# A linear-attention and gated-unit layer on one core: rewritten engine orders, in which x of tiles 0 and 1 is asked for between the two parts of the value weights

## The chip, the core and the metric

The kernel runs on one core of a Trainium2 chip. Its time is in device microseconds (us). The median of three runs before the change is 283.45 us (283.43 to 284.15). One more execution was profiled; all rows of the profile are of that one.

## The reference

There are 2048 rows of x with 640 columns, all in bf16, and 32 heads of 20.

```python
x = A_x
h = x + A(layernorm(x), A_wqkv, A_w_phi, A_wo)
h2 = h + B(layernorm(h), B_w_gate, B_w_up, B_w_down)

# A: q, k, v = x @ wqkv, by heads
pq = einsum("bhsd,hdf->bhsf", q, w_phi); pk = the same of k
phi_q = concat(softmax(pq), softmax(-pq)); phi_k = the same of pk
kv = einsum("bhsf,bhsd->bhfd", phi_k, v); z = sum of phi_k over s
o = (phi_q @ kv) / (phi_q @ z + 1e-6); result o @ wo

# B: ((x @ w_gate) * (x @ w_up)) @ w_down
```

## The kernel before, in words

The rows are worked in 16 tiles of 128. Because the sum over phi_k needs all rows, the kernel first makes keys and values of all tiles, then the sum, then queries, attention output and the gated unit, in four blocks of four tiles.

The layer norm is folded into the weights. For the keys and the queries the product of wqkv's part with the block-diagonal w_phi (tile `Phi`) is made first, and each row's mean is taken out of the weights. The names that matter here are those of the units in the written orders:

- `in`: the first loads. They are w_phi (`Wrows`), the five blocks of key weights into `Wnat` (called c0 to c4 below; a part of the tile `phiqT`), the value weights into `Wp` in two parts (blocks 0-1 and blocks 2-4), and x of tiles 0 to 3, transposed while it is loaded, into `xT` (x0 to x3 below).
- `wk` and `x0` to `x4`: the key weights. Each block c is summed over its columns for the mean (`means`) and transposed on TensorE (`turn`, line 656); then five rounds multiply it with `Phi` and write `Wp`.
- `wv` and `c0` to `c4` in the DVE order: column sums of the value weights, in the two parts, and the taking out of the mean.
- `s0`, `s2`, `s4`, `s8`, `s12`: mean and square sum of the tiles of x, by two or four tiles. `s2` needs x2 and x3.
- `wm` and `y0` to `y4`: the means of the query weights (`wq_means`, line 721), and five rounds with `Phi` (`wq_round`, line 728). They need `lwq`, the query weights in `Wnat`, and `t0` to `t4`, the same weights transposed by load into `WT`.
- `k`, `v`, `q`: ten matmuls of 320 columns for a tile's keys, values or queries; `K` and `Q` the rest of their softmax, with a large product on POOL each; `A` the sum over phi_k on TensorE.
- `n`, `h`, `f`, `d`, `e`: attention, output product, gated unit, down product.
- `lT4` to `lT15`: transposed loads of x for the other tiles. `lx0` to `lx3`: plain loads of x, four tiles each. `lg`, `lu`, `ld`: the gate, up and down weights, 1.92 MB each. `lwo`: the output weights, 0.8 MB.

What sets the order of the work: `ORDER` (line 58) holds a written list of units for each of the engines PE, DVE, ACT, POOL and SP. An engine issues its operations exactly in that list's order; operations of one unit on one engine are taken in the order in which the program makes them. `Prog.place` (line 200) walks the lists with a model of durations; from the walk come the buffer numbers and the slots of the DMA semaphores. The model's landing time of a load does not change the list. `Prog.finish` adds the waits. Loads go round a ring of eight semaphores (`"w"` for plain loads, `"tr"` for transposing loads), so a load waits for the eighth one before it on its ring. An engine that waits for an operation at the head of its list issues nothing behind it, and that holds for SP's loads too.

SP's list before begins with eleven `in` units (the five key blocks, the two value parts, x0 to x3), then `lT4 lT5 lT7 lT6 lx3 lT8 ...`. Loads issued by SP have line 465 (plain) and line 469 (transposing) in the profile before; matmuls made by the helper `mms` have line 568.

Of the kernel before, what the change touches and what calls it, by code (L numbers as in the profile page):

```python
# [5 lines left out]
FP32 = mybir.dt.float32  # L6
# [5 lines left out]
P = 128  # L12
# [60 lines left out]
    "DVE":  # L73
# [12 lines left out]
    "ACT":  # L86
# [9 lines left out]
    "POOL":  # L96
# [37 lines left out]
class Op:  # L134
    __slots__ = ("eng", "idx", "emit", "deps", "dma", "waits", "vc", "signal", "tick", "sem", "val",
                 "n", "dur", "lat", "bufs", "succ", "start", "end", "open", "bytes", "unit")


class Prog:
# [13 lines left out]
    def op(self, eng, emit, rd=(), wr=(), app=(), dma=None, t=0.2, lat=None, use=(), after=(), size=0.0):  # L153
        o = Op()
        o.eng, o.emit, o.dma = eng, emit, dma
# [44 lines left out]
    def place(self):  # L200
# [20 lines left out]
        while len(order) < len(ops):  # L221
# [29 lines left out]
            if o.dma is not None:  # L251
                land = max(s + 2.3, fabric) + o.bytes
                fabric = land
                o.end = land + o.lat
                flight.setdefault(o.dma[0], []).append(o.end)
            else:
                o.end = s + o.lat
# [119 lines left out]
def _build(ctx, nc, A_x, A_wqkv, A_w_phi, A_wo, B_w_gate, B_w_up, B_w_down, out):  # L377
# [43 lines left out]
    nmean = sb([P, NC], FP32, "nmean")  # L421
    Ssum = sb([P, 2, 2 * H], FP32, "Ssum")
# [9 lines left out]
    nmu, nmuk = [outb[:, k, :].rearrange("p (a n) -> p a n", a=NC) for k in range(2)]  # L432
# [31 lines left out]
    def load(out_, in_, wr, mb, after=(), eng="SP", app=()):  # L464
        return g.op(eng, lambda e: e.dma_start(out_, in_), wr=wr, app=app, after=after, dma=("w", 8), t=0.5, lat=0.4, size=mb / 0.38)  # L465

    def transpose(out_, in_, rd, wr, use=(), t=1.27, size=1.07):

        return g.op("SP", lambda e: e.dma_start_transpose(out_(), in_()), rd=rd, wr=wr, use=use, dma=("tr", 8), t=t, lat=0.5,  # L469
                    size=size)  # L470
# [27 lines left out]
    def load_wnat(w, cs=(0, NC), eng="SP"):  # L498
        c0, c1 = cs
        load(Wnat[:, c0:c1, :], A_wqkv[P * c0:P * c1, D * w:D * (w + 1)].rearrange("(c p) n -> p c n", p=P), R_Wnat[c0:c1],  # L500
             0.16 * (c1 - c0), eng=eng)

    def load_xT(t):
        transpose(lambda: xT[:, t, :, 0:P], lambda: A_x[0, P * t:P * (t + 1), :], [], [R_xT[t]], t=1.27, size=0.8 if t < 2 else 1.4)

    def load_x(b):
        load(x_all[:, 4 * b:4 * b + 4, :], A_x[0, 4 * P * b:4 * P * (b + 1), :].rearrange("(t p) n -> p t n", p=P), [R_x[b]], 0.64)

    def load_wv(c0, c1):
        load(Wp[:, c0:c1, 2 * D:3 * D], A_wqkv[P * c0:P * c1, 2 * D:3 * D].rearrange("(c p) n -> p c n", p=P), R_Wp[2][c0:c1], 0.16 * (c1 - c0))  # L510

    U("in")
    load(Wrows[:, :, :], A_w_phi.rearrange("h d f -> (h d) f").rearrange("(a p) f -> p a f", p=P), [R_Wrows], 0.03, eng="ACT")
    for c in range(NC):
        load_wnat(1, (c, c + 1))
    load_wv(0, 2)
# [587 lines left out]
```

## Time and profile before

| what | us |
|---|---|
| median of three runs | 283.45 |
| the profiled execution | 281.24 |
| its span, first to last instruction | 279.42 |
| TensorE busy | 274.6 |
| TensorE's first long run begins | 13.70 |
| last matmul done | 275.99 |
| DVE / ACT / POOL busy | 165.5 / 133.4 / 106.3 |

The page of the profile gives busy times, the span in 40 slices, the DMA queues, the chain of work that ended last, and the costliest groups. The chain of waits is followed back from the last instruction: at each step to what released it, or to the instruction before it on its engine. SPq is SyncE issuing a DMA. In a line of the list of waits the three numbers are the microseconds in all, how often, and the longest. In a line of the DMA issues the last number is the median time from issue to landing. In a line of the timeline the first two numbers are the start and the length in us.

### The profile page before, as it was taken

Reading aid. Unit: us, or ns where it says so; the run is one execution under the profiler, and the core shown is the slowest. Engines: PE = TensorE matmul, PEld = TensorE weight load, DVE = VectorE, ACT = ScalarE, POOL = GpSimd, SP = SyncE. Lnnn points to the kernel's source line nnn. Section 1 sums busy time; section 2 is a strip of 40 time slices with the busy share of each in tenths; the row PEclk is TensorE's granted clock in tenths of the full one; section 3 lists DMA queues with packets and bytes.
Section 4 is the critical chain, followed back from the end, with each engine's and each line's share of the span. In section 5 each row is a group of like instructions: output and inputs, shape, how many; then the busy total and the mean of one; then the engine's idle time right before and its main releaser. Section 6 shows DMA issues by size and latency. Waiting matters only on the chain.

```text
span 279.4 us, 5540 instructions
## 1 busy us (share of the span) xinstructions
PE 274.6 (98%) x2257; PEld 187.7 (67%) x2257; DVE 165.5 (59%) x313; ACT 133.4 (48%) x227; POOL 106.3 (38%) x156
## 2 busy tenths in 40 slices
PE   8999999999999999999999999999999999999996
PEld 7777778778878888877746655676454444456773
DVE  2999999999899798688528474431141132315011
ACT  2477999998566346363271432401444342410321
POOL 5348899999620322233300680002521034000321
PEclk9999999999999999999999999999999999999999
DMA  7989989404964378946530065561210001000112
GB/s 192 166 170 140 214 125 397 137 2 94 302 78 94 74 180 150 280 99 91 122 73 2 7 136 72 116 98 45 72 49 0 0 0 49 0 0 2 70 48 72
DMA packets 65241, 28.08 MB, mean 100 GB/s; under 512 B 55744, under 2 KB 63936, under 8 KB 65216
## 3 DMA queue, kind: packets, MB, share of 16 engines
q1 hardware_dynamic: 64560, 27.70, 45.8%
q8 instruction: 18, 0.29, 0.5%
q10 hardware_dynamic: 656, 0.03, 0.2%
q14 instruction: 7, 0.06, 0.1%
HBM read 11.82 MB, written 2.62 MB: 52 GB/s over the span
## 4 chain that ended last, share of the span: by engine, by line
PE 94%; SPq 3%; DMA 2%; DVE 1%; issue 0%
PE ps L568 93%; SPq L469 2%; DMA xT<-in_A_x_dram 2%; SPq L465 1%; PE ps L480 0%; DVE outb L1010 0%; DVE KVsb L893 0%; DVE rden L927 0%; DVE KVsb L896 0%
## 5 line engine op out<-in xcount | busy, mean ns | idle before, releaser
L568 PE MATMUL ps<-phik,Wgu 128*128 128x512 bf16 (+1 forms) x600 | 107.6, 336 | 0.0
L568 PEld LDWEIGHTS ps<-phik,Wgu 128*128 128x128 bf16 x600 | 58.2, 98 | 43.6 <-DVE phik L969 1.2
L969 DVE TENSOR_TENSOR phik<-ps,gate 128x512 bf16<-128x512 f32 (+1 forms) x60 | 34.0, 575 | 61.2 <-PE ps L568 60.3
L568 PE MATMUL ps<-Wp,xT 128*128 128x320 bf16 x480 | 68.4, 299 | 0.0
L967 ACT ACTIVATE gate<-ps 128x512 bf16<-128x512 f32 (+1 forms) x60 | 30.1, 512 | 70.4 <-PE ps L568 56.5
L568 PE MATMUL ps<-vaug,phik 128*128 128x320 bf16 (+3 forms) x544 | 60.2, 270 | 0.0
L568 PEld LDWEIGHTS ps<-Wp,xT 128*128 128x128 bf16 x480 | 46.2, 98 | 17.1
L568 PEld LDWEIGHTS ps<-vaug,phik 128*128 128x128 bf16 x544 | 43.4, 97 | 15.9
L985 POOL TENSOR_TENSOR outb<-t,x_all 128x640 bf16<-128x640 f32 x12 | 16.8, 1397 | 88.0 <-ACT t L982 85.7
L827 POOL TENSOR_TENSOR phik<-phik,Rk 128x1280 bf16<-128x1280 bf16 x16 | 37.3, 2357 | 0.7 <-DVE nb L809 0.6
L982 ACT ACTIVATE t<-ps,mh,rs 128x640 f32<-128x640 f32 x12 | 10.6, 882 | 41.4 <-PE ps L568 41.4
L806 DVE TENSOR_REDUCE ps<-ps 128x1 f32<-128x640 f32 x32 | 26.2, 819 | 3.5 <-PE ps L568 3.1
L846 DVE TENSOR_REDUCE Sq<-eq 128x64 f32<-128x1280 bf16 x16 | 23.5, 1474 | 1.6 <-ACT eq L813 1.6
L824 DVE TENSOR_REDUCE Ssum<-phik 128x64 f32<-128x1280 bf16 x16 | 23.4, 1471 | 0.1
L857 POOL TENSOR_TENSOR eq<-eq,rq 128x640 bf16<-128x640 bf16 x16 | 20.3, 1270 | 0.9
L852 POOL TENSOR_TENSOR rq<-Sq,rq 128x32 f32<-128x32 f32 x16 | 4.0, 255 | 39.8 <-DVE rq L851 39.8
L813 ACT ACTIVATE eq<-ps,nb,rs 128x640 bf16<-128x640 f32 x16 | 14.1, 883 | 10.1 <-DVE nb L809 9.3
L813 ACT ACTIVATE phik<-ps,nb,rs 128x640 bf16<-128x640 f32 x16 | 14.0, 884 | 3.1 <-DVE nb L809 3.0
L561 ACT ACTIVATE junk<-x_all 128x640 bf16<-128x640 bf16 x20 | 14.7, 735 | 0.0
L833 ACT ACTIVATE vaug<-ps,rs 128x640 bf16<-128x640 f32 x16 | 12.8, 801 | 3.5 <-PE ps L568 3.5
L813 ACT ACTIVATE eq<-ps,nb,nrs 128x640 bf16<-128x640 f32 x16 | 14.1, 882 | 0.0
L946 DVE SCALAR_TENSOR_TENSOR x_all<-ps,mh,x_all 128x640 bf16<-128x640 f32 x16 | 13.9, 874 | 0.4
(83 smaller groups left out, 226.4 us busy)
## 6 DMA issues: line engine op xcount, KB each, us to landing
x_all<-in_A_x_dram SPq DMA_DIRECT2D x4, 640.0 KB, 9.0
out_dram<-outb SPq DMA_DIRECT2D x15, 160.0 KB, 1.8
Wgu<-in_B_w_up_dram SPq DMA_DIRECT2D x1, 1920.0 KB, 11.3
Wgu<-in_B_w_gate_dram SPq DMA_DIRECT2D x1, 1920.0 KB, 8.2
vaug<-in_B_w_down_dram SPq DMA_DIRECT2D x1, 1920.0 KB, 8.5
phiqT<-in_A_wqkv_dram SPq DMA_DIRECT2D x5, 160.0 KB, 3.8
phiqT<-in_A_wqkv_dram SPq DMA_DIRECT2D x1, 800.0 KB, 6.0
Wo<-in_A_wo_dram SPq DMA_DIRECT2D x1, 800.0 KB, 5.6
```

The source lines that it names most:

```text
L561: g.op("ACT", lambda e: e.activation(out=junk[:, v.i, :], in_=in_, func=func, accum_out=acc), rd=rd, wr=wr, use=[v], t=0.73, lat=0.97)
L568: ins = e.matmul(o_, lhsT=l_, rhs=r_, start=s_, stop=p_, skip_group_check=True)
L806: g.op("DVE", lambda e: e.tensor_reduce(out=mx(), in_=PS[v.i][:, :, 0:HALF], axis=AX.XY, op=ALU.max, apply_absolute_value=True, negate=Tru ...
L813: g.op("ACT", lambda e, s=s, sc=sc: e.activation(out=signed(dst(), s), in_=PS[v.i][:, :, 0:HALF].rearrange("p b (h f) -> p b h f", f=DH), ...
L824: g.op("DVE", lambda e: e.tensor_reduce(out=Ssum[:, vs.i, :], in_=x, axis=AX.X, op=ALU.add), rd=R_phik[t], wr=vs.R, use=[vs], t=1.39, lat=1.5)
L827: g.op("POOL", lambda e: e.tensor_tensor(out=x, in0=x, in1=Rk[:, vr.i, :].unsqueeze(2).to_broadcast([P, 2 * H, DH]), op=ALU.mult), rd=vr.R ...
L846: g.op("DVE", lambda e: e.tensor_reduce(out=Sq[:, vs.i, :], in_=eq[:, b.i, :].rearrange("p (g f) -> p g f", f=DH), axis=AX.X, op=ALU.add), ...
L857: return e.tensor_tensor(out=x, in0=x, in1=rq[:, vr.i, :].unsqueeze(2).to_broadcast([P, H, DH]), op=ALU.mult)
L946: g.op("DVE", lambda e: e.scalar_tensor_tensor(out=xv, in0=PS[v.i][:, :, 0:HALF], scalar=mh[:, t:t + 1], in1=xv, op0=ALU.subtract, op1=ALU ...
L967: g.op("ACT", lambda e: e.activation(out=gate[:, vg.i, 0:P * n], in_=PS[v.i][:, 0, 0:P * n], func=ACT.Copy), rd=[v.R[0]], wr=vg.R, use=[v, ...
L969: g.op("DVE", lambda e: e.tensor_tensor(out=hhT[:, hb, ft, sl], in0=PS[v.i][:, 1, 0:P * n], in1=gate[:, vg.i, 0:P * n], op=ALU.mult), rd=[ ...
L985: g.op("POOL", lambda e: e.tensor_tensor(out=outb[:, vo.i, :], in0=t32[:, v3.i, :], in1=x_all[:, t, :], op=ALU.add), rd=v3.R + [R_h[t]], w ...
```

## The change

1. All five written lists in `ORDER` are new.
2. The first loads are made in another order, and key blocks 2 and 3 go as one load over ACT's queue. In the program x of tiles 0 and 1 now stands between the two parts of the value weights. In SP's new list the eleven `in` units are nine, and they no longer stand together at its head.
3. `load` and `transpose` take a landing time `at`; where it is given, the planner's model uses it as the landing, whenever the load is issued. (`at` stands in the model alone.)
4. `lwq`, `lwo` and the last `lx` are issued by ACT instead of SP.
5. The mean of the query weights: ACT writes five numbers (`nmeanq`) instead of a 640-wide tile, five operations on POOL (`wq0` to `wq4`) add them to the transposed weights, and the rounds `y` on TensorE leave their second half out.

SP's and the beginning of PE's list, before (-) and after (+), and the rest of the diff's core:

```diff
     "PE":
-        "warm wk wk wk wk wk wk wk wk wk wk x1 wv x1 x0 x3 wv x0 s0 s0 x2 x4 k0 k0 k0 s2 k0 k0 s2 k1 k3 v1 k2 s4 s4 s4 s4 "
+        "warm wk wk wk wk wk wk wk wk wk wk x1 wv x1 s0 x2 s0 x3 x4 wv x0 x0 s2 s2 wm k1 k0 k0 k0 k0 k0 s4 s4 s4 s4 s8 s8 "
...
     "POOL":
+        "in in in in in in in in in in in in in in in in in in wk in s0 in s0 s0 in s0 s0 wq4 in in s0 s2 in s2 s4 s2 wq1 "
+        "s2 s4 s4 s2 s2 s4 s4 s8 wq3 s8 s4 s0 s8 s8 s8 K1 s8 K3 wq2 s2 K0 wq0 s8 K2 s12 s12 s12 s12 K4 s12 K7 K8 s12 K11 "
...
     "SP":
-        "in in in in in in in in in in in lT4 lT5 lT7 lT6 lx3 lT8 lT11 lT10 lT9 lT15 t0 lT13 lwq t3 lT12 t2 t4 t1 lT14 "
-        "lwo lu lx0 lx2 Q0 Q0 Q1 Q1 lg Q2 Q2 Q3 Q3 Q5 Q5 n2 n3 Q7 Q7 h2 h3 Q6 Q6 lx1 Q4 Q4 n5 ld n6 n7 h5 Q8 Q8 Q9 n4 Q9 "
+        "in t4 lT10 lT8 lT7 lT5 lT11 lT4 lT6 lT9 t1 in t3 lg in lT15 in t2 in in lu t0 lT14 lT13 in in lT12 lx0 in Q1 lx2 "
+        "Q0 Q1 Q0 Q2 Q2 Q3 Q3 Q5 Q5 n2 n3 Q6 Q6 h2 h3 Q4 lx1 Q4 n6 n5 Q7 Q7 Q9 n4 Q9 ld h5 n7 Q10 n9 Q10 h4 h7 h6 Q12 Q12 "
...
-                land = max(s + 2.3, fabric) + o.bytes
+                land = o.at or max(s + 2.3, fabric) + o.bytes
...
     U("in")
-    load(Wrows[:, :, :], A_w_phi.rearrange("h d f -> (h d) f").rearrange("(a p) f -> p a f", p=P), [R_Wrows], 0.03, eng="ACT")
-    for c in range(NC):
-        load_wnat(1, (c, c + 1))
-    load_wv(0, 2)
-    load_wv(2, 5)
-    for t in range(4):
-        load_xT(t)
+    load(Wrows[:, :, :], A_w_phi.rearrange("h d f -> (h d) f").rearrange("(a p) f -> p a f", p=P), [R_Wrows], 0.03, eng="ACT", at=3.3)
+    load_wnat(1, (0, 1), at=3.0)
+    load_wnat(1, (2, 4), "ACT", at=4.8)
+    load_wnat(1, (1, 2), at=3.7)
+    load_wnat(1, (4, 5), at=5.3)
+    load_wv(0, 2, 6.2)
+    load_xT(0, 6.2)
+    load_xT(1, 6.9)
+    load_wv(2, 5, 9.3)
+    load_xT(2, 9.2)
+    load_xT(3, 9.9)
...
-        g.op("ACT", lambda e: e.activation(out=nmu[:, :, :], in_=PS[v.i][:, 0, 0:NC].unsqueeze(2).to_broadcast([P, NC, P]),
-                                           func=ACT.Copy, scale=-1.0 / SC), rd=[v.R[0]], wr=[R_nmu], use=[v], t=0.61, lat=0.75)
+        g.op("ACT", lambda e: e.activation(out=nmeanq[:, :], in_=PS[v.i][:, 0, 0:NC], func=ACT.Copy, scale=-1.0 / SC),
+             rd=[v.R[0]], wr=[R_nmu], use=[v], t=0.1, lat=0.23)
+        for a in range(NC):
+            U("wq%d" % a)
+            pool_op(lambda e, a=a: e.tensor_scalar(out=WT[:, 0, a, :], in0=WT[:, 0, a, :], scalar1=nmeanq[:, a:a + 1], scalar2=None,
+                                                   op0=ALU.add), 0.75, rd=[R_nmu, R_WT[0][a]], wr=[R_WT[0][a]])
...
-        g.op("PE", lambda e: mms(e, part(WT[:, 0, :, P * i:P * (i + 1)], first) + part(nmu, first)), rd=R_WT[0] + R_Phi + [R_nmu],
-             wr=v.R, use=[v], t=0.62, lat=0.77)
+        g.op("PE", lambda e: mms(e, part(WT[:, 0, :, P * i:P * (i + 1)], first)), rd=R_WT[0] + R_Phi,
+             wr=v.R, use=[v], t=0.31, lat=0.46)
...
-    load_wnat(0)
+    load_wnat(0, eng="ACT")
...
-    load(Wo[:, :, 0:D], A_wo.rearrange("(c p) n -> p c n", p=P), R_Wo, 0.8)
+    load(Wo[:, :, 0:D], A_wo.rearrange("(c p) n -> p c n", p=P), R_Wo, 0.8, eng="ACT")
```

More of the change, by code (lines that the diff above doesn't have):

```diff
@@ L135 @@
     __slots__ = ("eng", "idx", "emit", "deps", "dma", "waits", "vc", "signal", "tick", "sem", "val",
-                 "n", "dur", "lat", "bufs", "succ", "start", "end", "open", "bytes", "unit")
+                 "n", "dur", "lat", "bufs", "succ", "start", "end", "open", "bytes", "unit", "at")
 class Prog:
@@ L151, in __init__, with op @@
         self.order = {}
-    def op(self, eng, emit, rd=(), wr=(), app=(), dma=None, t=0.2, lat=None, use=(), after=(), size=0.0):
+    def op(self, eng, emit, rd=(), wr=(), app=(), dma=None, t=0.2, lat=None, use=(), after=(), size=0.0, at=0.0):
         o = Op()
+        o.at = at
         o.eng, o.emit, o.dma = eng, emit, dma
@@ L421, in _build @@
     nmean = sb([P, NC], FP32, "nmean")
+    nmeanq = sb([P, NC], FP32, "nmeanq")
     Ssum = sb([P, 2, 2 * H], FP32, "Ssum")
@@ L431, in _build @@
     WT = pq[:, NC * D:3 * NC * D].rearrange("p (w a n) -> p w a n", w=2, a=NC)
-    nmu, nmuk = [outb[:, k, :].rearrange("p (a n) -> p a n", a=NC) for k in range(2)]
+    nmuk = outb[:, 1, :].rearrange("p (a n) -> p a n", a=NC)
     vaug = BV[:, :].rearrange("p (t h e) -> p t h e", t=NT, h=H)
@@ L462, in _build, with load, transpose @@
     R_hT, R_oT, R_hhT = [regs(4) for _ in range(2)], [regs(4) for _ in range(2)], [[regs(4) for _ in range(NF)] for _ in range(2)]
[L464 to L470, printed above, removed]
+    def load(out_, in_, wr, mb, eng="SP", at=0.0):
+        return g.op(eng, lambda e: e.dma_start(out_, in_), wr=wr, dma=("w", 8), t=0.5, lat=0.4, size=mb / 0.38, at=at)
+    def transpose(out_, in_, rd, wr, use=(), t=1.27, size=1.07, lat=0.5, at=0.0):
+        return g.op("SP", lambda e: e.dma_start_transpose(out_(), in_()), rd=rd, wr=wr, use=use, dma=("tr", 8), t=t, lat=lat,
+                    size=size, at=at)
     def transpose_pe(out_, in_, rd, wr, use, v, bk):
@@ L494, in U, with load_wnat, load_xT, load_wv @@
         g.unit = name
-    def load_wnat(w, cs=(0, NC), eng="SP"):
+    def load_wnat(w, cs=(0, NC), eng="SP", at=0.0):
         c0, c1 = cs
         load(Wnat[:, c0:c1, :], A_wqkv[P * c0:P * c1, D * w:D * (w + 1)].rearrange("(c p) n -> p c n", p=P), R_Wnat[c0:c1],
-             0.16 * (c1 - c0), eng=eng)
-    def load_xT(t):
-        transpose(lambda: xT[:, t, :, 0:P], lambda: A_x[0, P * t:P * (t + 1), :], [], [R_xT[t]], t=1.27, size=0.8 if t < 2 else 1.4)
+             0.16 * (c1 - c0), eng=eng, at=at)
+    def load_xT(t, at=0.0):
+        transpose(lambda: xT[:, t, :, 0:P], lambda: A_x[0, P * t:P * (t + 1), :], [], [R_xT[t]], t=1.3, size=0.75, lat=1.25, at=at)
     def load_x(b):
-        load(x_all[:, 4 * b:4 * b + 4, :], A_x[0, 4 * P * b:4 * P * (b + 1), :].rearrange("(t p) n -> p t n", p=P), [R_x[b]], 0.64)
-    def load_wv(c0, c1):
-        load(Wp[:, c0:c1, 2 * D:3 * D], A_wqkv[P * c0:P * c1, 2 * D:3 * D].rearrange("(c p) n -> p c n", p=P), R_Wp[2][c0:c1], 0.16 * (c1 - c0))
+        load(x_all[:, 4 * b:4 * b + 4, :], A_x[0, 4 * P * b:4 * P * (b + 1), :].rearrange("(t p) n -> p t n", p=P), [R_x[b]], 0.64,
+             eng="ACT" if b == NB - 1 else "SP")
+    def load_wv(c0, c1, at):
+        load(Wp[:, c0:c1, 2 * D:3 * D], A_wqkv[P * c0:P * c1, 2 * D:3 * D].rearrange("(c p) n -> p c n", p=P), R_Wp[2][c0:c1], 0.16 * (c1 - c0), at=at)
     U("in")
-    load(Wrows[:, :, :], A_w_phi.rearrange("h d f -> (h d) f").rearrange("(a p) f -> p a f", p=P), [R_Wrows], 0.03, eng="ACT")
-    for c in range(NC):
-        load_wnat(1, (c, c + 1))
-    load_wv(0, 2)
-    load_wv(2, 5)
-    for t in range(4):
-        load_xT(t)
+    load(Wrows[:, :, :], A_w_phi.rearrange("h d f -> (h d) f").rearrange("(a p) f -> p a f", p=P), [R_Wrows], 0.03, eng="ACT", at=3.3)
[9 more added lines that the diff above has]
+    load_xT(3, 9.9)
     def pool_op(f, t, **k):
@@ L1019, in wqT @@
         U("t%d" % a)
-        transpose(lambda: WT[:, 0, a, :], lambda: A_wqkv[:, P * a:P * (a + 1)], [], [R_WT[0][a]], t=1.27, size=1.4)
+        transpose(lambda: WT[:, 0, a, :], lambda: A_wqkv[:, P * a:P * (a + 1)], [], [R_WT[0][a]], t=1.5, size=0.75, lat=1.25)
     U("warm")
```

78 rows, old and new, of the table ORDER are left out of this document.

## The prediction

> **What bounds the kernel now.** I read the page first: the busy line and the clock row.
>
> ```profile
> PE 274.6 (98%) x2257; PEld 187.7 (67%) x2257; DVE 165.5 (59%) x313; ACT 133.4 (48%) x227; POOL 106.3 (38%) x156
> PEclk9999999999999999999999999999999999999999
> ```
>
> TensorE is busy for 98% of the span at a full granted clock; no other engine is near it. The chain of waits, in order of time, says the same and gives the dates that I use:
>
> ```profile
> 4.12 1.30 SPq L469
> 5.47 1.26 SPq L469
> 6.77 2.20 SPq L469
> ...
> 9.02 4.64 DMA xT<-in_A_x_dram
> 13.65 0.05 issue
> 13.70 62.00 PE ps L568 x670
> ...
> 85.88 190.10 PE ps L568 x1312
> 275.99 0.03 issue
> ```
>
> Until 13.65 the chain is SyncE issuing loads; the last one that counts is x of tile 3 (tile "x3" below), issued at 9.02, landed at 13.65. From 13.70 to 275.99 it is TensorE with under a microsecond of other work (the copy of KV at 75.7). So **the time is a start, then 262.29 us of TensorE, then 3.43 us** (279.42 - 275.99). Whatever delays TensorE's first long run is paid in full, since TensorE has no idle time later to pay it back from. TensorE's waits are short indeed:
>
> ```profile
> PE ps L568 <- POOL ones L525: 1.0, 1, 1.0
> PE ps L568 <- DVE KVsb L896: 0.6, 1, 0.6
> PE ps L568 <- DMA phiqT<-in_A_wqkv_dram: 0.3, 1, 0.3
> ```
>
> SyncE's timeline gives the price of an issue:
>
> ```profile
> 0.79 2.29 SPq L465 DMA_DIRECT2D phiqT<-in_A_wqkv_dram  x5
> 3.12 0.95 SPq L465 DMA_DIRECT2D Wp<-in_A_wqkv_dram  x2
> 4.12 12.38 SPq L469 DMA_TRANSPOSE xT<-in_A_x_dram  x8
> 16.55 0.59 SPq L465 DMA_DIRECT2D x_all<-in_A_x_dram  x1
> 17.18 7.85 SPq L469 DMA_TRANSPOSE xT<-in_A_x_dram  x5
> ```
>
> A plain load holds SyncE for 0.43 to 0.6. A transposing load holds it for 1.2 to 2.2: the 21 from DRAM took 32.49, so 1.55 each, 1.59 with the gap.
>
> **The change, part by part.**
>
> *The order of SyncE's queue* decides. Before, SyncE issues all eleven "in" loads first (five blocks of key weights c0 to c4, two parts of value weights, x0 to x3). After, its list reads: c0, t4, eight x tiles (10 8 7 5 11 4 6 9), t1, **c1**, t3, gate weights lg (1.92 MB), **c4**, lT15, **value weights 0-1**, t2, **x0**, **x1**, lu (1.92 MB), t0, lT14, lT13, **value weights 2-4**, **x2**, lT12, lx0 (0.64 MB), **x3**. The landing times now written into these loads (at=) steer the planner's model only; they move no instruction. TensorE's list still begins with all blocks c0 to c4, then x1, value sums, s0 (x0, x1), the second value sums, s2 (x2, x3), the means wm, and only then the keys. Nothing on TensorE may pass a waiting instruction, and DVE, ACT and POOL live on what TensorE makes. So the first key tile starts after x3 has landed.
>
> When is that? Up to lg, SyncE's issue is the limit: 1.24 + 10 x 1.59 = 17.1; c1 0.47, t3 1.59: lg is issued at 19.2. From there the queue's order of landing is the limit, by these rows:
>
> ```profile
> Wgu<-in_B_w_up_dram SPq DMA_DIRECT2D x1, 1920.0 KB, 11.3
> x_all<-in_A_x_dram SPq DMA_DIRECT2D x2, 640.0 KB, 12.9
> Wo<-in_A_wo_dram SPq DMA_DIRECT2D x1, 800.0 KB, 5.6
> ```
>
> They were issued at 38.22 (Wo), 39.07 and 39.64 and landed at 43.8, 50.4 and about 52.1: each behind the one before. So 1.92 MB takes 6.5 us, 0.295 MB/us. The gate weights alone took 8.2 from issue. Transposes queued behind a load (issued at 17.18, 18.45, 19.76, landed 7.0, 6.3 and 5.6 later; two more at 28.34 and 29.61, landed 5.9 and 5.4 later) came 0.55 to 0.76 apart: 0.65.
>
> lg lands at 19.2 + 8.2 = 27.4, or, behind t3 (issued at 17.6, landed 4.7 later as its like), at 22.3 + 6.5 = 28.8; I take 28.3. Then c4 0.54, lT15 0.65, value part one 1.08, t2, x0, x1 1.95: 32.5. lu 6.5: 39.0. Three transposes 1.95, value part two 1.63, x2 and lT12 1.3, lx0 2.17, x3 0.65: 46.7. Beside these the query weights lwq (0.8 MB) now come from ACT's queue; ACT may issue them only when TensorE has read c4, so they fall into this stretch and share the same engines. No row shows two loaded queues: 0 if they fit in, 3.9 if they come in whole (before, 29.8 to 33.7). I take 0.8 / 0.295 = 2.7. **x3 lands at 49.4.** With the second s2 (0.29) and wm (0.63) the keys begin at **50.3**.
>
> A rule of the Trainium skill speaks against the moves to ACT's queue (Trainium Kernel Development and Optimization, Key Constraints): loads issued from several engines run on the same 16 DMA engines, and only issue time is saved. No run here shows it; by it lwq, the third x load and Wo buy nothing but SyncE's 0.6 each, and the sum stays.
>
> *What TensorE has left from there.* Of its 262.29, s2 (0.29) and wm (0.63) are already done, and ten matmuls of k0 that before ran by 13.70 are still to do (40 such take 5.43, so 1.36). The five query rounds lose their second half (mean part):
>
> ```profile
> 41.84 0.47 PE L568 MATMUL ps<-Phi,phiqT 128*128 128x140 bf16 x6
> 42.15 0.48 PE L568 MATMUL ps<-Phi,outb 128*128 128x140 bf16 x6
> 42.47 0.48 PE L568 MATMUL ps<-Phi,phiqT 128*128 128x140 bf16 x6
> ```
>
> Each half holds TensorE from 42.15 to 42.47: 0.315, five times 1.58. Left: 262.29 - 0.29 - 0.63 - 1.58 + 1.36 = 261.15.
>
> *A cold array.* TensorE's first 26 matmuls of 128 columns took 2.95, 113 ns each; later 320 columns take 136 ns, 54 per 128. The slow stretch lasted from 1.04 to about 6.2. Whether a pause brings it back no row shows: 0, or up to half of 5.2, 2.6. The new start has pauses longer than all of before's work up to the keys, so I take 1.5, nearer the slow row. The Trainium skill (TensorE: Matmul & The Clock Gate, part 1) says that one idle window of about 3.4 us halves the clock until a busy window has passed; that is an estimate of 1.7, and the sum would be 0.2 more.
>
> *Five additions on POOL* (the mean, now added to the transposed query weights; ACT's copy goes from 640 to 5 wide, which nothing waits for). Nearest rows: 0.72 (L686, 640 wide) to 1.27 (L857), so 3.6 to 6.4. Three stand ahead of POOL's first key product, where POOL was half idle before (5.73 busy of the 11.30 us to 25.0); two stand between the key products, where it was 14.15 of 15.00 busy. The last key product ended at 72.03 while TensorE was already in the sum over phik (from 71.72), so there is about a microsecond of cover. 0 to 4; I take 1.
>
> The other new orders (queries, gates) I cost at nothing: TensorE had no waits there, and its list holds the same matmuls; other orders there could add, at most about the KV copy's 0.9 again.
>
> *The sum.* 50.3 + 261.15 + 1.5 + 1 + 3.43 = 317.4 as span; the profiled execution is 1.82 longer than its span (281.24 to 279.42): 319.2, so +38.0. The median of the runs, 283.45, is 2.2 above the profiled one; the same step on it gives **321.5**.
>
> **The rivals.**
>
> *The loads don't keep the order.* Small loads might overtake lg and lu. Then SyncE's issue alone counts: from lg at 19.2 it needs nine loads and transposes before x3, in all 19.2 to issue x3's end (ten transposes at 1.59, six loads at 0.5 to 0.6), 38.4, landed at 41.6 (4.8 after issue): 7.8 less, 313.7; with every transpose at its shortest, 1.28, 21 x 0.27 less again: 308. Against: all the landings read above came in the order of issue. For: the Trainium skill (DMA: Bandwidth & Descriptors, Queues, rings and completion order) says completion need not be in order on one issuing engine.
>
> *Issue and transfers press on each other.* ACT now sends 1.76 MB (third x load, c2-3, Wo) in the first microseconds. If each of the eleven transposes ahead of lg takes the longest row, 2.2, lg comes 6.7 later; if lg takes lu's 11.3 instead of 9.1, 2.2 more; 330, and 333 with POOL's upper end.
>
> *Faster after all.* TensorE loses 1.58 us of matmuls, and if its start stayed at 13.7 the time would be 283.45 - 1.6 = 281.9. The place is the wait for c4; it decides only if c4, both value parts and x3 land by 13.65. Eleven transposes stand ahead of c4, none in the trace below 1.2: 13.2 before it can be issued. That the written order is not what runs is the same rival.
>
> **How the numbers follow.** Forecast 0.62 (316 to 328), loads overtake 0.17 (308 to 314), pressure 0.18 (328 to 336), faster 0.02, within 0.3% 0.01 (0.3%, 0.85 us, is about what a measurement of this kernel tells from no change). The range 309 to 334 leaves out the edges of both. Faster 0.02, same 0.01, slower 0.97.
>
> **What would show it.** TensorE idle in the first 50 us with waits on the phiqT, Wp and xT loads, above all until c1 (about 20), c4 (28.8), value part two (about 45) and x3 (49); the first ten-matmul key tile near 50; from there to the last matmul 262 to 265; c4 landing right after lg (28 to 29) and x3 some 21 after lg. Wrong if c4 lands before lg, if the keys begin before 40, or if TensorE idles over 4 us after them.

## The result, and the profile after

Six runs of the changed kernel have a median of **322.62 us** (321.93 to 325.07), six of the kernel before 283.44 (281.68 to 284.15): 1.1408 times the time, 95% interval 1.1355 to 1.1461. The profiled run took 322.54, its span is 320.8. One run below, of the kernel that fills the pause, is 1.6% above the fastest of that kernel and is left out of its figures as a slow run.

The page of the changed kernel: busy time of each engine with its share of the span, TensorE's busy tenths and its granted clock in 40 slices of 8.02 us each.

```profile
PE 280.9 (88%) x2227; PEld 190.6 (59%) x2227; DVE 165.5 (52%) x313; ACT 133.0 (41%) x227; POOL 116.9 (36%) x161
...
PE   4024248996999999999999999999999999999996
...
PEclk9999757998999999999999999999999999999999
```

TensorE has 30 matmuls fewer, yet 6.3 us more busy time: some of it ran slowly. Six slices with a 0 to 4 in them are the start; the 6 behind them and the clock's 8 fall in one slice, 72 to 80 us, and are a second loss. The list of TensorE's waits (in all, times, longest):

```profile
PE ps L575 <- DMA phiqT<-in_A_wqkv_dram: 21.0, 2, 15.4
PE ps L575 <- DMA Wp<-in_A_wqkv_dram: 10.3, 2, 10.1
PE ps L575 <- POOL phiqT L736: 2.1, 1, 2.1
PE ps L575 <- DMA xT<-in_A_x_dram: 1.7, 1, 1.7
...
PE ps L575 <- ACT phik L824: 0.4, 1, 0.4
```

Line 568 of before is line 575 here; L736 is the new addition of the mean. The three DMA rows are waits for c1 (15.4) and c4 (5.6), for the second part of the value weights, and for x3. The chain in order of time (start, length, what):

```profile
42.99 0.58 SPq L467
43.61 5.34 DMA xT<-in_A_x_dram
49.00 6.62 PE ps L575 x70
...
61.63 1.88 POOL phiqT L736
...
75.51 1.88 POOL phiqT L736
77.44 39.48 PE ps L575 x415
116.94 0.58 DVE KVsb L904
...
182.44 134.94 PE ps L575 x814
317.41 1.02 DVE outb L1021 x2
```

Before, SyncE's issuing held the chain to 9.02 us, then x3's transfer to 13.65, and x3 released TensorE; now x3 is issued at 43.61 and lands at 48.95. The keys begin at 49.92. Between 56 and 77 us the chain goes through POOL, which it did not before. From the copy of KV on it is TensorE again.

Three dates divide each kernel: the first key tile, the copy of KV (line 896 before, 904 after), and the end of the span.

| kernel | keys begin | keys to KV copy | KV copy to the end |
|---|---|---|---|
| before (from 13.70) | 13.70 | 62.0 | 203.7 |
| predicted for after | 50.3 | 63.4 | 203.7 |
| after | 49.92 | 67.0 | 203.9 |

The predicted middle is 62.0 less the 1.14 of work that is gone, plus 1.5 and 1. So 36.2 us came in at the start, 5.0 in the middle, and nothing behind it, although all five lists were rewritten to their ends.

### The profile page after: what moved, and what is told of

The parts are those of the page before. It is cut to its first block, busy times and chain, and to the rows that moved or that the text cites. A ratio compares the mean times of both kernels' runs of the same rounds, so it can differ in the third digit from the quotient of the medians.

```text
span 320.8 us, 5473 instructions
## 1 busy us (share of the span) xinstructions
PE 280.9 (88%) x2227; PEld 190.6 (59%) x2227; DVE 165.5 (52%) x313; ACT 133.0 (41%) x227; POOL 116.9 (36%) x161
## 4 chain that ended last, share of the span: by engine, by line
PE 72%; SPq 13%; POOL 7%; DMA 3%; issue 2%; DVE 1%; ACT 1%; ACTq 0%
PE ps L575 72%; SPq L471 12%; POOL phiqT L736 2%; POOL phik L838 2%; DMA xT<-in_A_x_dram 2%; DMA phiqT<-eq 1%; SPq L467 1%; POOL rs L631 1%; POOL eq L868 0%; PE ps L482 0%; DVE outb L1021 0%; ACT eq L824 0%; DVE x_all L957 0%; ACT t L993 0%; POOL vpe L629 0%
## 5 line engine op out<-in xcount | busy, mean ns | idle before, releaser
L575 PE MATMUL ps<-Wp,xT 128*128 128x320 bf16 x480 | 71.7, 307 | 0.5 <-ACT phik L824 0.4
L575 PEld LDWEIGHTS ps<-Wp,xT 128*128 128x128 bf16 x480 | 47.0, 100 | 19.6 <-ACT phik L824 0.9
L868 POOL TENSOR_TENSOR eq<-eq,rq 128x640 bf16<-128x640 bf16 x16 | 20.3, 1271 | 1.1
L575 PE MATMUL ps<-ones,phiqT 128*128 128x1 bf16 x50 | 2.3, 167 | 21.0 <-DMA phiqT<-in_A_wqkv_dram 21.0
L963 POOL TENSOR_SCALAR vpe<-shc 128x1 f32<-128x1 f32 x16 | 3.1, 192 | 39.2 <-ACT junk L568 38.4
L575 PEld LDWEIGHTS ps<-ones,phiqT 128*128 128x128 bf16 x50 | 2.0, 104 | 21.8 <-DMA phiqT<-in_A_wqkv_dram 21.8
```

The lines of the kernel that those rows point to most:

```text
L575: ins = e.matmul(o_, lhsT=l_, rhs=r_, start=s_, stop=p_, skip_group_check=True)
L868: return e.tensor_tensor(out=x, in0=x, in1=rq[:, vr.i, :].unsqueeze(2).to_broadcast([P, H, DH]), op=ALU.mult)
```

## The experiments

**Theory A**: the start is SyncE's list. The transposing loads and the two weight loads of 1.92 MB that now stand among the `in` loads set x3's landing, and TensorE's written order, with all the column sums ahead of the keys, turns that date into the end. **Rivals**: the pause itself costs (a slow clock), the middle costs (POOL's additions), or the edit that the title names, x0 and x1 between the two parts of the value weights, costs. The ratios are to the kernel before, run beside each group. The changed kernel itself gave medians of 322.62 and, run once more with the last group, 321.25: a difference of under 1.4 us from it shows nothing by itself.

### The nine loads at the head again

```diff
-        "in t4 lT10 lT8 lT7 lT5 lT11 lT4 lT6 lT9 t1 in t3 lg in lT15 in t2 in in lu t0 lT14 lT13 in in lT12 lx0 in Q1 lx2 "
+        "in in in in in in in in in t4 lT10 lT8 lT7 lT5 lT11 lT4 lT6 lT9 t1 t3 lg lT15 t2 lu t0 lT14 lT13 lT12 lx0 Q1 lx2 "
```

> The changed kernel with one edit: SyncE's list has all nine first loads (in) at its head, the rest of the list unchanged. Theory A (the start is late because these loads stand behind transposes and the gate and up weights): x of tile 3 lands at about 14 to 16 instead of 48.95, the keys begin near 16, but the next loads are now late by the same cause: s4 waits for lT6 (about 25) some 7 us and s12 for lT12 behind lu (about 47); time 290 to 300. Theory B (the new lists of the other engines and the five POOL additions are what costs): time above 315. Theory C (the start is all of it, nothing follows): 284 to 288.

Measured 297.23 (296.99 to 297.47), 1.0506 [1.041, 1.0602]. So 25.4 of the 39.2 us hang on SyncE's list alone, in the range that A gave; but the dates inside were not A's. x3 landed at 19.24, not at 14 to 16, although only first loads stood ahead of it on SyncE: ACT had sent lx3, c2-3, Wo and then lwq, 2.56 MB, beside them. (In the start put right by hand, below, lx3 and Wo are out of the way, the same nine loads stand first, and x3 landed at 11.27: ACT's loads are what held it back.) So the keys began at 20.21, 6.5 later than before's long run. And from there to the copy of KV it took 71.9, longer than in either kernel. TensorE's waits show why:

```profile
PE ps L575 <- DMA xT<-in_A_x_dram: 5.3, 4, 2.7
PE ps L575 <- DMA phiqT<-in_A_wqkv_dram: 3.9, 3, 1.9
PE ps L575 <- DVE sxx L619: 2.5, 1, 2.5
PE ps L575 <- POOL phiqT L736: 2.1, 1, 2.1
```

The transposed x tiles are asked for in the order 10 8 7 5 11 4 6 9, and TensorE needs 4 to 7 first (`s4`): behind an early start they come late. The third row is a chain of its own: POOL's second addition waited for t1 at the head of POOL's list, with the row statistics behind it.

```profile
31.90 1.89 POOL L736 TENSOR_SCALAR phiqT<-phiqT,nmeanq 128x640 bf16<-128x640 bf16 x1 [3.35 <-DMA phiqT<-in_A_wqkv_dram]
```

The bracket says that POOL stood idle for 3.35 us before it. In the changed kernel these costs hide behind the later start.

### The edit of the title undone

```diff
     load_wv(0, 2, 6.2)
+    load_wv(2, 5, 9.3)
     load_xT(0, 6.2)
     load_xT(1, 6.9)
-    load_wv(2, 5, 9.3)
```

> The changed kernel with one edit: in the program both parts of the value weights come before x of tiles 0 and 1, so that in SyncE's list value part two takes the place of x0, x0 that of x1, and x1 comes behind lu where value part two was. Theory A (only the landing of the last first load, x3, sets the start): x3 lands as before the edit within 1 us, time within 1 us of the changed kernel's 322.6. Theory B (the place of x0 and x1 between the value parts is itself a cost or a gain): more than 1.5 us either way.

Measured 322.16 (321.31 to 323.86), 1.1395 [1.1318, 1.1472]. The wait moved from Wp (10.3 to 0.2) to xT (1.7 to 11.3), x3 landed at 49.63, and the time is the same. As A said, the edit costs nothing here: x3 is last whichever comes first.

### The gate and up weights behind x3

```diff
-   "... t1 in t3 lg in lT15 in t2 in in lu t0 lT14 lT13 in in lT12 lx0 in Q1 lx2 "
+   "... t1 in t3 in lT15 in t2 in in t0 lT14 lT13 in in lT12 lx0 in lg lu Q1 lx2 "
```

> The changed kernel with one edit: the gate and up weights (lg, lu, 3.84 MB) go behind x3 in SyncE's list. Theory A (loads land in the order of their queue, so 3.84 MB are ahead of x3): x3 lands near 39 instead of 48.95 and is then limited by issue, time 312 to 314. Theory B (small loads do not wait for the large ones; the transposes' issue is all): x3 lands within 3 us of 48.95, time above 319.

Measured 313.95 (313.22 to 314.68), 1.1097 [1.0992, 1.1202]. x3 landed at 40.51 and the keys began at 41.74: 8.2 earlier, and the time is 8.7 less. The two loads of 1.92 MB cost about 8 of the 36 us, not their 13 of transfer: without them SyncE's transposes, issued in turn, become the limit.

### Four loads early, x left behind

```diff
-        "in t4 lT10 lT8 lT7 lT5 lT11 lT4 lT6 lT9 t1 in t3 lg in lT15 in t2 in in lu t0 ...
+        "in in in in t4 lT10 lT8 lT7 lT5 lT11 lT4 lT6 lT9 t1 t3 lg lT15 t2 in in lu t0 ...
```

> The changed kernel with one edit: c1, c4 and the first part of the value weights are issued with c0 at the head of SyncE's list; x0, x1, value part two, x2 and x3 stay where they are. This removes TensorE's two longest waits on the key weights (15.4 and 5.7 us in the list of waits). Theory A (only the landing of x3 counts): the waits move to the later loads, x3 lands between 46 and 49.5 (the query weights, which now load earlier, give up to 2.7), time 319 to 323. Theory B (each listed wait is a price of its own): about 21 us less, 300 to 304.

Measured 320.37 (319.53 to 321.78), 1.1314 [1.123, 1.1398]. This kernel shows how little a list of waits says of gain:

```profile
PE ps L575 <- DMA xT<-in_A_x_dram: 20.7, 2, 18.8
PE ps L575 <- DMA Wp<-in_A_wqkv_dram: 7.5, 1, 7.5
PE ps L575 <- DMA phiqT<-in_A_wqkv_dram: 3.5, 3, 1.7
```

The wait for c1 and c4 fell by 17.5 and that for Wp by 2.8, and the time by 2.2 (by 0.8 between the profiled runs): x0's row took them over. Only x3's landing, 48.02 for 48.95, counts. It also separates lwq's share: ACT sent lwq early here, and from the issue of lg to x3 it took 26.08 instead of 30.07, 3.99 less, of which 1.62 are c4 and value part one that no longer stand there. The other 2.4 I put down to lwq; that is a difference, not a row.

### Filling the pause

```diff
...
+            if c0 == 0:
+                g.op("PE", lambda e: mms(e, [(PS[v.i][:, 0, HALF:HALF + P], ones[:, :], ones[:, :], False, False) for _ in range(130)]),
+                     rd=[R_one], wr=v.R, use=[v], t=9.0, lat=9.1)
...
```

> The changed kernel with 130 more matmuls of the constant tile into unused PSUM columns, which nothing reads, put on TensorE between the first and the second part of the value sums, where it waits from about 34 to 44. Theory A (after the long waits TensorE runs at about half speed for a stretch, and that is paid after x3): the granted clock after 44 is 1.0, the first twenty key matmuls take 2.7 to 2.9 instead of 4.4, time 1.5 to 2.5 less than the changed kernel, 320 to 321. Theory B (the other engines set the pace right after the start): the clock rises but the time stays within 0.7 us of 322.6.

Measured 320.62 (three runs, 320.32 to 323.15), 1.1387 [1.1324, 1.1451]. That lies in the range of A, but the changed kernel's own two medians, 322.62 and 321.25, differ by more than the 0.6 to it: no gain is shown. The first two key tiles of the changed kernel, then those of this one with the stretch before them, in TensorE's timeline (start, length, what, number of matmuls, idle time before):

```profile
49.92 4.55 PE L575 MATMUL ps<-Wp,xT 128*128 128x320 bf16 x20
```

```profile
34.22 7.47 PE L575 MATMUL ps<-ones 128*128 128x128 bf16 x130
45.08 1.78 PE L575 MATMUL ps<-Wp,ones 128*128 128x320 bf16 x6 [3.40 <-DMA Wp<-in_A_wqkv_dram]
...
49.87 2.88 PE L575 MATMUL ps<-Wp,xT 128*128 128x320 bf16 x20
52.59 2.15 PE L575 MATMUL ps<-xT 128*128 128x129 bf16 x35
55.54 1.53 PE L575 MATMUL ps<-Wp,xT 128*128 128x320 bf16 x10 [0.81 <-ACT phik L827]
```

Twenty matmuls took 2.88 instead of 4.55: 1.67 gained. But the third tile begins 0.75 earlier only, since ACT then holds it for 0.81. And the fill did not do it as meant: behind its end at 41.69 came a wait of 3.40, and the six matmuls at 45.08 are slow again (1.78, against 0.98 for the same six in the first experiment). Four kernels with no fill at all, the changed kernel run once more among them (last experiment), had a profiled run that was warm at this place.

### The additions on DVE

```diff
-            pool_op(lambda e, a=a: e.tensor_scalar(out=WT[:, 0, a, :], in0=WT[:, 0, a, :], scalar1=nmeanq[:, a:a + 1], ...
+            g.op("DVE", lambda e, a=a: e.tensor_scalar(out=WT[:, 0, a, :], in0=WT[:, 0, a, :], scalar1=nmeanq[:, a:a + 1], ...
...
-        "... K0 k8 K2 k8 k6 K4 k6 K7 K4 k10 ...
+        "... K0 k8 wq4 wq1 K2 k8 k6 wq3 K4 k6 wq2 wq0 K7 K4 k10 ...
```

> The changed kernel with the five additions of the query means (1.88 us each on POOL) moved to DVE, spread between its key products, and taken out of POOL's list. Theory A (POOL's 9.4 us are why TensorE waits 2.1 us for the query rounds, and the slow clock right behind that wait is a part of it): the wait and the slow stretch at 77 to 80 go, time 3 to 4.5 less, 318 to 319.5. Theory B (DVE is as full as TensorE in the key stage, so the price only moves): within 1 us of 322.6. DVE's price by its nearest row (0.41 for 384 wide out of PSUM) is 0.25 to 0.7 each.

Measured 324.14 (323.38 to 324.48), 1.1482 [1.1435, 1.1529]: A missed. The rival had the direction, that the price only moves, but not the size: it allowed 1 us, and this is 1.5 above 322.6. The wait for L736 is gone; a wait of 3.4 for ACT's exp (phik) has come, the longest 2.3, with slow matmuls behind it. DVE's timeline, and POOL's for the same time:

```profile
69.68 2.20 DVE L736 TENSOR_SCALAR phiqT<-phiqT,nmeanq 128x640 bf16<-128x640 bf16 x2
...
73.02 1.95 DVE L736 TENSOR_SCALAR phiqT<-phiqT,nmeanq 128x640 bf16<-128x640 bf16 x1
...
76.35 0.67 DVE L736 TENSOR_SCALAR phiqT<-phiqT,nmeanq 128x640 bf16<-128x640 bf16 x2
```

```profile
72.43 2.35 POOL L838 TENSOR_TENSOR phik<-phik,Rk 128x1280 bf16<-128x1280 bf16 x1 [0.75 <-DVE nb L820]
```

Two additions took 0.67 with POOL idle, 0.33 each. One that began while POOL's product ran, from 72.43 to 74.78, took 1.95 and ended at 74.97, 0.19 after it: DVE waited for POOL's instruction to end. The Trainium skill (SBUF — State Buffer, SBUF: two separate sides) says this: GpSimd and VectorE share a pair of ports, and an operation of GpSimd, or one of VectorE in a mode that uses the pair, holds it for the whole instruction and blocks the other. The rows agree.

### The kernel before with the mean on DVE

The kernel before, with five numbers for the mean, the additions on DVE, and the rounds' second half left out:

```diff
-        g.op("PE", lambda e: mms(e, part(WT[:, 0, :, P * i:P * (i + 1)], first) + part(nmu, first)), ...
+        g.op("PE", lambda e: mms(e, part(WT[:, 0, :, P * i:P * (i + 1)], first)), ...
...
+        "... K6 k9 wq0 wq3 wq2 K8 k10 wq4 wq1 K5 ...
```

> The kernel before with one part of the change alone: the query means are added to the transposed weights (by DVE, five operations between its key products) and the second half of the query rounds is gone from TensorE; all lists else and all loads as before. Theory A (TensorE is the only bound): 1.6 us less than before, 281.0 to 281.9 where before is 282.6 to 283.4. Theory B (DVE, busy 19.34 of 20 us there, takes the place of the gain): between 0.5 less and 2 more.

Measured 286.41 (284.28 to 287.63), 1.0145 [1.0102, 1.0189]: slower, outside A and above the rival's upper end. TensorE has 1.58 us less to do and, where the additions stand, one new wait.

```profile
PE ps L569 <- DVE phiqT L730: 3.1, 1, 3.1
```

Three of the additions fell on POOL's products again and took 3.40 together. The edit that removes work gives back twice its worth as a wait. The profiled run also has a late start (its first key matmuls stand at 15.27, before's at 11.73); from these to the copy of KV it took 66.7, against 64.0 before. So 2.7 us belong to the stretch with the additions, and whether the late start belongs to the edit this one profile can't show.

### A start put right by hand

Several edits at once: SP's list as below, lwo later on ACT and lx3 on SP, the additions on DVE, tiles 0 and 1 swapped, and `wm`, `s12` and the pieces of Wo moved to where they hold nothing.

```diff
+        "in in in in in in in in in lT4 lT5 lT7 lT6 lx3 lT8 lT11 lT10 lT9 lT15 t4 t1 lT13 t3 lT12 t2 lT14 t0 lx0 lu lg Q1 lx2 "
```

> The changed kernel with all nine first loads at the head of SyncE's list, the other x tiles in the order of need behind them, the third x load on SyncE and Wo later on ACT's list, the gate and up weights behind all x tiles, and the query means added by DVE; the other lists of the change stay but for places of wm, s12 and wo that follow from the loads. Theory A (the start, POOL's additions and the cold clock are all that the change cost): x3 lands at 13 to 15, time 280.5 to 284. Theory B (the new lists of PE, DVE and POOL cost something of their own): 285 to 292.

Measured 296.76 (294.74 to 298.1), 1.0501 [1.0452, 1.0551]: longer than either theory gave. The start was right: x3 landed at 11.27, the keys began at 14.67. Then TensorE waited, and ran slowly between:

```profile
PE ps L575 <- ACT phik L824: 4.3, 4, 2.3
PE ps L575 <- DMA xT<-in_A_x_dram: 4.0, 2, 2.4
PE ps L575 <- DVE nb L820: 1.7, 2, 1.2
PE ps L575 <- DMA phiqT<-in_A_wqkv_dram: 1.3, 1, 1.3
```

Keys to KV copy took 76.8, against 67.0 in the changed kernel. Whether the change's lists or the places that were patched in by hand cause this stays open; with so many edits the kernel can't tell.

### POOL's additions made short

```diff
-            pool_op(lambda e, a=a: e.tensor_scalar(out=WT[:, 0, a, :], in0=WT[:, 0, a, :], ...
+            pool_op(lambda e, a=a: e.tensor_scalar(out=WT[:, 0, a, 0:16], in0=WT[:, 0, a, 0:16], ...
```

> The changed kernel with the five additions on POOL made 16 columns wide instead of 640; the mean of the other query weight columns is left out of the computation. Theory A (POOL's 9.4 us cause TensorE's 2.1 us wait for the query rounds and the slow clock behind it): wait gone, clock 1.0 there, 3 to 4 less than the changed kernel, 318.5 to 319.5. Theory B (another engine's wait takes its place at once, as with the additions on DVE): less than 1 us gained.

Measured 318.28 (317.22 to 320.28), 1.1269 [1.1217, 1.1321], 2.97 less than the changed kernel in the same group (321.25). This isolates the cost of POOL's additions. The group's line (busy, mean ns) in the changed kernel and here:

```profile
L736 POOL TENSOR_SCALAR phiqT<-phiqT,nmeanq 128x640 bf16<-128x640 bf16 x5 | 9.5, 1898 | 13.3 <-ACT nmeanq L732 13.3
```

```profile
L736 POOL TENSOR_SCALAR phiqT<-phiqT,nmeanq 128x16 bf16<-128x16 bf16 x5 | 1.7, 339 | 13.4 <-ACT nmeanq L732 13.4
```

And the stretch from 75 to 82 us, in the changed kernel and here (length; busy time and number of TensorE's matmuls, of its weight loads, DVE, ACT, POOL; clock, DMA share, GB/s):

```profile
75.00:82.00 7.00, 4.89 (x51) 3.60 (x48) 5.09 (x9) 4.25 (x8) 6.83 (x9) 0.76 0.00 0
```

```profile
75.00:82.00 7.00, 7.00 (x75) 5.47 (x73) 7.00 (x12) 6.21 (x12) 5.98 (x7) 1.00 0.00 0
```

With the short additions TensorE is busy throughout at full clock, and its wait for L736 is gone. Keys to KV copy took 62.56 here, with no wait of TensorE in it: the 60.9 of work and 1.6 of a cold first key tile (4.45 in this run).

The slow clock behind the wait is the small part of what the additions cost. Seven of the profiled runs have that wait, of 2.1 each. In four (the changed kernel both times, the weights behind x3, four loads early) the next matmuls were slow, and from the end of the wait to the copy of KV it took 39.3 to 39.5. In three (the first two experiments and the filled pause) the clock stayed at 1.00 there, as in the row of the values put together, and it took 39.03 to 39.04:

```profile
75.00:82.00 7.00, 4.98 (x55) 3.93 (x56) 5.41 (x9) 5.68 (x11) 6.83 (x9) 1.00 0.00 0
```

So the slow stretch costs 0.2 to 0.5; where it is missing, TensorE waits 0.6 for ACT further on. Keys to KV copy took 65.4 and 65.5 in the filled pause and with the values together, both with a warm first tile and no slow stretch. Less its cold tile this kernel took 61.0: by the profiles the additions on POOL cost some 4.4 us, by the medians 3.0.

### The additions on ACT, in both kernels

```diff
...
-            pool_op(lambda e, a=a: e.tensor_scalar(out=WT[:, 0, a, :], in0=WT[:, 0, a, :], scalar1=nmeanq[:, a:a + 1], scalar2=None,
-                                                   op0=ALU.add), 0.75, rd=[R_nmu, R_WT[0][a]], wr=[R_WT[0][a]])
+            g.op("ACT", lambda e, a=a: e.activation(out=WT[:, 0, a, :], in_=WT[:, 0, a, :], func=ACT.Identity, bias=nmeanq[:, a:a + 1]),
+                 rd=[R_nmu, R_WT[0][a]], wr=[R_WT[0][a]], t=0.7, lat=0.83)
```

> The changed kernel with the five additions of the query means on ACT (0.7 us each by the activations of 640 columns), spread between its key work, with three of the wo sums moved later. Theory A (the additions hurt because POOL is full and slow at them): 2 to 4 less than the changed kernel, 318.5 to 320.5. Theory B (ACT, 14.9 of 18 us busy between 57 and 75, then holds the key tiles): 322 to 325.

> The kernel before with the query means added by ACT, the second half of the query rounds gone, the rounds one key tile later in TensorE's list and three wo sums later in ACT's; loads and all else as before. Theory A (ACT shares nothing with POOL and has room, so TensorE's 1.58 us come through): 0.8 to 1.6 less than before. Theory B (ACT, 33.4 of 35 us busy between 25 and 60, is as full as TensorE): 0 to 3 more than before.

In the changed kernel 323.53 (321.1 to 324.54), 1.1453 [1.1408, 1.1499], no faster than the 321.25 beside it. An addition costs ACT 871 ns, and TensorE then waits 3.0 for ACT's exp:

```profile
L736 ACT ACTIVATE phiqT<-phiqT,nmeanq 128x640 bf16<-128x640 bf16 x5 | 4.2, 871 | 0.0
```

In the kernel before 288.44 (287.01 to 290.25), 1.0204 [1.0164, 1.0243]: slower, above the range that the rival gave. TensorE waits 2.4 for the additions and 1.5 for the exp; its profiled run, too, begins its keys late, at 12.97. ACT, DVE and POOL each have idle time over the whole span, but whichever of the three got the additions, TensorE waited in this stretch.

### The changed kernel once more

> The changed kernel once more, as a control on the same chip as the runs beside it: 322 to 323.5. If the clock record shows a slow stretch right behind the wait for the query rounds again, that stretch belongs to the kernel; if it is at 1.0 there, it was chance.

Measured 321.25 (320.16 to 323.47), 1.1371 [1.1324, 1.1418]. This is a little below the 322 to 323.5 that I expected. The first key tiles took 2.88, warm, with a profiled run of 320.89 against 322.54. Keys to KV copy took 65.65 against 67.0, so of the 1.67 of that tile 1.3 came through. The wait of 2.1 for L736 was the same, and so was the clock behind it:

```profile
75.00:82.00 7.00, 5.90 (x53) 4.56 (x54) 4.54 (x8) 4.49 (x9) 6.83 (x9) 0.76 0.00 0
```

So the slow first key tile comes and goes from run to run, and the wait for L736 stays. None of these kernels beats the one before.

## Why the prediction was right, and which terms were off

**What bounds it: right.** A later start was paid in full, and behind the copy of KV no kernel of this study but one differs by over 0.3 us from the 203.7 of before (the one with four loads early has 204.1).

**The start: right to 0.4 us, step by step.** SyncE's timeline of the changed kernel and its DMA issues (the last number is the time from issue to landing):

```profile
2.52 13.19 SPq L471 DMA_TRANSPOSE xT<-in_A_x_dram  x8
...
18.88 0.58 SPq L467 DMA_DIRECT2D Wgu<-in_B_w_gate_dram  x1
19.51 0.52 SPq L467 DMA_DIRECT2D phiqT<-in_A_wqkv_dram  x1
...
29.31 0.58 SPq L467 DMA_DIRECT2D Wgu<-in_B_w_up_dram  x1
29.93 2.93 SPq L471 DMA_TRANSPOSE phiqT<-in_A_wqkv_dram  x1
32.91 6.85 SPq L471 DMA_TRANSPOSE xT<-in_A_x_dram  x2
```

```profile
Wgu<-in_B_w_gate_dram SPq DMA_DIRECT2D x1, 1920.0 KB, 8.6
Wgu<-in_B_w_up_dram SPq DMA_DIRECT2D x1, 1920.0 KB, 11.2
...
phiqT<-in_A_wqkv_dram ACTq DMA_DIRECT2D x1, 800.0 KB, 7.6
```

| date | predicted | measured |
|---|---|---|
| lg issued | 19.2 | 18.88 |
| lg landed | 28.3 | 27.53 |
| c4 landed | 28.8 | 27.96 |
| x1 landed | 32.5 | 31.24 |
| lu landed | 39.0 | 40.47 |
| x3 landed | 49.4 | 48.95 |
| keys begin | 50.3 | 49.92 |

Two errors inside it cancel in part. Transfers up to x1 were 1.3 faster than I took, and from lu to x3 they took 8.5 instead of 7.7. lu was 2.7 slower than in the table, and it is there that ACT sent lwq (28.89, landed 36.50), for which the sum holds 2.7 beside the dates; the experiment with four loads early gives 2.4. And SyncE did not issue freely behind the large loads: a transpose at 29.93 held it 2.93, one of the next two 4.33. This cost nothing, since those transfers stood behind lu anyway.

**The Trainium skill's rule on loads from several engines: right.** (Trainium Kernel Development and Optimization, Key Constraints.) With the nine loads at SyncE's head x3 lands at 19.24 with lx3, Wo and lwq on ACT's queue beside them, and at 11.27 in the start put right by hand, where lx3 and Wo come later and lwq is issued at 8.90. The move to ACT saved no transfer time.

**The rivals.** Small loads did not overtake: c4 landed 0.43 after lg, and in all fourteen profiled runs every load from DRAM on SyncE's queue landed in the order of issue, so the rule of the Trainium skill that completion need not be in order (DMA: Bandwidth & Descriptors, Queues, rings and completion order) showed nothing here. Issue and transfers pressed little: of the ten transposes ahead of c1 one took 3.23, above the longest row of before, the others 1.2 to 1.7. "Faster after all" had no ground. (The prediction's "nine loads and transposes before x3" are fourteen; its sum counts them all.)

**A cold array: the term was 1.5, it measured 1.3 to 1.7.** The first twenty key matmuls cost 1.67 extra in the profiled run, near the 1.5 that I took, and 1.3 of it reached the copy of KV. The estimate of 1.7 by the Trainium skill (TensorE: Matmul & The Clock Gate, part 1) agrees for that run. That it was there at all is luck: of nine profiled runs with the late start, four had a slow first tile (4.0 to 4.6) and five a warm one (2.88). A second slow stretch followed, behind the wait for L736 (ten matmuls from 78.58 took 2.75 where their like take 1.52). That I did not foresee: I priced the clock once, at the pause I had in view, and not at each wait that the change adds. It cost 0.5 at most, as the runs without it show. The Trainium skill speaks on that page of an idle window of about 3.4 us that runs free of the kernel. The slow first tile that comes and goes would fit a window whose phase differs from run to run. The Trainium skill doesn't say there that a wait of 2.11 suffices; it did in four of the seven profiled runs with that wait. What decides is open.

**POOL's additions: the term was 1, it measured 3.0 to 4.4.** This term is the step that was mis-sized. The price of one instruction was wrong: I bounded it by 0.72 and 1.27 from POOL rows of the same width, and it took 1.88 to 1.9, above both ends, 9.5 in all. The cover of a microsecond that I named lies at the last key product, and TensorE's waits came before it. In the two runs with a warm tile and no slow stretch it waits 2.1 for the additions and 1.4 for ACT, and its matmuls take some 0.8 longer than with short additions (61.8 against 62.6 less 1.6 for the cold tile). The additions save 1.58 us of matmuls; shortened, they gave 2.97 back.

**One of the prediction's own signs failed.** From the first key tile to the last matmul it gave 262 to 265; 267.5 came (49.92 to 317.38), the 5.0 of the middle against the 1.4 forecast there.

**From the span to the median: +2.2 predicted, +0.1 measured.** Before's profiled run, 281.24, was faster than all six others, and I carried its distance from the median over. After's was a run with the cold first tile, in the middle of its own. So the span came out 3.4 longer than predicted and the step 2.1 shorter: the two nearly cancel, and the closeness of 321.5 to 322.62 is better than the working behind it.

## What to carry to other kernels

A load's place in a queue is its date: sum what stands ahead of it, by issue where loads are small and by transfer where they are large, and look for the one load that the critical engine's first long run needs; removing waits ahead of that one moves them and gains little. Moving work off a full engine pays only if the engine that takes it has time in that very stretch, and needs the duration of that very form of instruction, not that of a like one. A slow stretch that shows in a profile is not yet a price: what it costs is read from a like run without it.

## What the runs showed of the hardware that was not expected

- A one-input addition on POOL (128x640 bf16, a number per partition) took 1.90 us; POOL's product of two inputs of that size (L868) takes 1.27. On DVE the addition took 0.33 alone and up to 1.95 beside POOL, on ACT 0.87.
- A wait of TensorE of 2.1 us was followed by slow matmuls (a granted clock of 0.63 to 0.67 over the next 4.5 to 5 us) in four profiled runs, the changed kernel's two among them, and not in three others with the same wait.
- In fourteen profiled runs all loads from DRAM issued by SyncE landed in the order of issue.
- With lx3, Wo and lwq on ACT's queue beside SyncE's nine first loads x3 landed at 19.24; with lx3 and Wo taken away and lwq issued at 8.90 it landed at 11.27.
- A transposing load issued behind a load of 1.92 MB held SyncE for up to 4.33 us in the changed kernel and 6.17 with the values together, against 1.2 to 1.3 at the shortest; the plain loads among them in the changed kernel took 0.52 to 0.58.
